# One more half-batch through VectorE and DMA, a state that decays inside PSUM, and a new order for every task of an attention-plus-mixer kernel

## The chip, the cores and the metric

The program runs on one core of a Trainium2 chip. The core has five engines with instruction streams of their own: TensorE (PE in the profile; its weight loads are listed apart as PEld), VectorE (DVE), ScalarE (ACT), GpSimd (POOL) and SyncE (SP), which here only starts DMAs. The metric is the time of one execution on the device in microseconds; lower is better. Each kernel is timed several times, and the median counts.

## The reference

The inputs are `r`, `k`, `v` of shape (4 batches, 8 heads, 768 tokens, 48), a decay `w` and a bonus `u` of shape (8, 48), and four weight matrices. All are float32, and so is the result of shape (4, 768, 384).

```python
for t in range(S):                                   # linear attention with a decaying state
    kt, vt, rt = (k[:, :, t], v[:, :, t], r[:, :, t])
    cur = np.einsum('bhd,bhe->bhde', u[None] * kt, vt)
    y[:, :, t] = np.einsum('bhd,bhde->bhe', rt, state + cur)
    state = w[None, :, :, None] * state + np.einsum('bhd,bhe->bhde', kt, vt)
...
xt = x.transpose(0, 2, 1)                            # x: the heads side by side, 384 wide
h = np.maximum(xt @ w_tok1, 0.0) @ w_tok2            # 768 -> 256 -> 768, along the tokens
u = x + h.transpose(0, 2, 1)
h2 = np.maximum(u @ w_ch1, 0.0) @ w_ch2              # 384 -> 1536 -> 384, along the channels
return u + h2
```

The `u` of the last lines is not the bonus: it is the sum of the attention's result and the token mixer's, and it is this sum that the change is about.

## The kernel before, in words

**Attention.** The 768 tokens of a batch are six units of 128 tokens. Within a unit the recurrence is turned into matrix products: `k` and `r` are multiplied by powers of `w` (tables `wnat`, `wpair`, `wp`), turned so that the channels lie on the partitions, multiplied with each other (`scores`, tile `at_ps`), masked by VectorE (`AT`), and multiplied with `v` (`outputs`, tile `y_ps`). The bonus is a separate product per head (`adg`, `yd`), and what earlier units hand on is a state of 48x48 per head, kept for two heads in one block of `kv_ps` (`state`). Batch 0 takes the units in pairs of neighbouring tokens (`pair_unit`, three windows of 256 tokens whose loads, tile `zr` or `win`, are 384 KB); batch 1 reads `r` in such windows and `k`, `v` by units; in batches 2 and 3 the scaled `k` and `r` are turned by a DMA on SP's queue (`turn_rk`).

**State.** The units of a batch are taken in groups of `GB[b]` = 2, 2, 3, 3. Inside a group the state grows in one PSUM bank (`kv_ps`), and each unit's predecessor state is copied out in bfloat16 by `keep_state`. At a group's end VectorE multiplies `kv_ps` by the decay of the whole group (`wGm`) into a tile `S0` in SBUF, and the next group begins with a product of the identity and that tile (task kinds `kv_id`, `kvw_id`), which brings the decayed state back into PSUM. There are six such ends: two each in batches 0 and 1, one each in 2 and 3.

**Mixers.** `mixer(b)` multiplies all six units of `x_b` by `wtok1` (`hidden`), takes the relu (`h1r`), and multiplies by `wtok2` (`back`). Then come two halves of three units each (`sg` 0 and 1). A half that is in `DIRECT` gets its sum `u`, channels on the partitions, wholly on PE: nine products of `x_b` with the identity turn it into `hx_ps` (`turn_x`), `back_T` adds the token mixer's part, ACT or VectorE copies the sum to `uT`, and at the very end nine more products with the identity add `uT` to the output (`down_res`). In a half that is not, `back` leaves tokens on the partitions (`hT_ps`), VectorE adds `x_b` and writes `u_sb` (`sum_u`), a DMA on SP's queue turns three units at once into `uT` (`turn_u`), and VectorE adds `u_sb` to the finished output (`sum_o`). After that both are alike: `up` makes 12 blocks `z_ps` of 1536 hidden channels (three products of 384 columns each), ACT or VectorE takes the relu into `zr`, `down` multiplies by `wch2` (tile `h_ps`, three calls of four products for each unit), and the result is stored. Batch 0 was direct in both halves, batch 1 in the first.

**Order.** Nothing is scheduled at run time. Every step is a task of class `Plan`, numbered in the order in which the code adds it; `ORDER` lists all task numbers, and `Plan.run` emits them so. Each engine therefore sees its own tasks in this order and waits for each in turn. `flex` tasks may run on one of two engines: `ENGINES` says on which. `BUFS` names the buffer that each tile takes, and a tile that takes a buffer waits until its last user is done. SP's loads stand in the same list and wait for their buffers in order; the seven pieces of the weights are DMAs of POOL, behind POOL's products.

**Zero products.** Tasks of kind `warm` multiply a tile of zeros into the unused part of PSUM bank `kv0`, as one product of 512 columns (those in `WIDE_AT`) or four of 128. Nothing waits for them. The wide ones write the whole bank and stand ahead of the first state product. Before there were 20 (10 wide).

Of the kernel before, what the change touches and what calls it, by code (L numbers as in the profile page):

```python
# [63 lines left out]
]  # L64
BUFS = {
    'AT0': [
# [1169 lines left out]
```

## Time and profile before

| | |
|---|---|
| Time, median of 3 runs | 161.94 us (161.71 to 162.23) |
| Span of the profiled execution | 160.1 us, first to last instruction |
| PE busy | 155.0 us, 97% of the span |
| VectorE busy | 116.0 us, 72% |
| ScalarE busy | 67.1 us, 42% |
| GpSimd busy | 79.0 us, 49% |
| Moved by DMA | 26.90 MB, 168 GB/s over the span |
| Granted TensorE clock | 0.997 |

The profile is of one execution, whose own span is 160.1 us; the timed median is 1.84 us above it. Busy time is the union of an engine's instructions. An engine's instructions overlap a little (products are pipelined), so a row's mean duration is longer than the step from one instruction to the next; the chain of waits gives the steps. A row of the timeline reads: start, duration, engine, line, operation, output from input, shapes, count. All operations come through one helper at line 279, so tiles, not lines, tell them apart.

### The profile page before, as it was taken

How to read it: one execution, taken by the hardware profiler on the slowest of the kernel's cores; microseconds unless marked ns; L12 is line 12 of the kernel's file. 1: busy time of each engine (PE TensorE's matmuls, PEld its weight loads, DVE VectorE, ACT ScalarE, POOL GpSimd, SP SyncE). 2: the span in 40 equal slices, each digit the busy share in tenths (PEclk: the TensorE clock that was granted, in tenths of full speed). 3: DMA queues.
4: the chain of work that ended last, by engine and by line, in shares of the span. 5: the costliest groups of instructions: out<-in, count | busy, mean ns of one | idle time of the engine just before them, and what ended most of it. 6: DMA issues, size and time to landing. Idle time of an engine off the chain costs nothing.

```text
span 160.1 us, 4053 instructions
## 1 busy us (share of the span) xinstructions
PE 155.0 (97%) x1617; PEld 105.7 (66%) x1618; DVE 116.0 (72%) x237; ACT 67.1 (42%) x149; POOL 79.0 (49%) x103
## 2 busy tenths in 40 slices
PE   6999999999999999999999999999999999999991
PEld 3577766777666777666667766676677666666670
DVE  4669995437866998879969988997797455445432
ACT  2859774976332465442316614234353200522100
POOL 7328899417145498434999917398972000000000
PEclk9999999999999999999999999999999999999998
DMA  5999999999998995899999999999961051620142
GB/s 129 262 261 244 218 233 190 198 208 195 229 212 151 188 197 112 186 153 201 207 231 152 236 131 250 220 216 151 196 168 53 0 123 26 197 84 17 49 147 98
DMA packets 86821, 26.90 MB, mean 168 GB/s; under 512 B 81554, under 2 KB 85908, under 8 KB 86804
## 3 DMA queue, kind: packets, MB, share of 16 engines
q1 hardware_dynamic: 84448, 23.40, 75.4%
q0 software_dynamic: 2160, 3.15, 11.5%
q8 instruction: 12, 0.20, 0.6%
q10 hardware_dynamic: 196, 0.11, 0.2%
q14 instruction: 5, 0.04, 0.1%
HBM read 20.46 MB, written 4.72 MB: 157 GB/s over the span
## 4 chain that ended last, share of the span: by engine, by line
PE 95%; DVE 1%; ACT 1%; issue 0%
PE h_ps L279 36%; PE z_ps L279 30%; PE kv_ps L279 8%; PE y_ps L279 6%; PE at_ps L279 4%; PE hT_ps L279 3%; PE hx_ps L279 3%; PE tr_ps L279 1%; PE w_ps L279 1%; PE trk L279 1%; ACT ka L279 1%; ACT rkb L279 1%; PE tk_ps L279 1%; PE u_ps L279 1%; PE ad_ps L279 0%; DVE pr L279 0%
## 5 line engine op out<-in xcount | busy, mean ns | idle before, releaser
L279 PE MATMUL h_ps<-wch,zr 128*128 128x384 bf16 (+1 forms) x300 | 55.0, 320 | 0.0
L279 PE MATMUL z_ps<-uT,wch 128*128 128x384 bf16 x288 | 52.0, 327 | 0.0
L279 ACT ACTIVATE zr<-z_ps 128x384 bf16<-128x384 f32 x52 | 23.6, 490 | 50.9 <-PE z_ps L279 50.8
L279 PEld LDWEIGHTS <-wch 128*128 128x128 bf16 x288 | 32.0, 114 | 13.9 <-DVE x_b L279 0.4
L279 PEld LDWEIGHTS <-zr 128*128 128x128 bf16 x300 | 27.0, 97 | 14.7
L279 DVE TENSOR_SCALAR zr<-z_ps 128x384 bf16<-128x384 f32 x44 | 23.1, 551 | 15.3 <-PE z_ps L279 15.2
L279 DVE TENSOR_TENSOR AT<-at_ps,mask 128x512 bf16<-128x512 f32 x36 | 23.2, 680 | 1.5 <-PE at_ps L279 1.5
L279 POOL TENSOR_TENSOR yd<-vb,adg 128x384 f32<-128x384 bf16 x15 | 12.6, 847 | 9.1 <-DVE vb L279 3.8
L279 POOL TENSOR_TENSOR ku<-kt,u_bc 128x384 f32<-128x384 f32 x11 | 11.0, 1001 | 11.9 <-DMA kt<-in_k_dram 9.8
L279 POOL TENSOR_TENSOR kr<-kt,wnat 128x384 bf16<-128x384 f32 x13 | 13.3, 1025 | 1.1 <-PE z_ps L279 1.0
L279 PEld LDWEIGHTS <-kr 128*128 128x128 bf16 (+1 forms) x196 | 11.7, 97 | 3.1 <-issue 0.4
L279 POOL TENSOR_TENSOR kr<-rt,wp 128x384 bf16<-128x384 f32 x10 | 10.6, 1069 | 3.1 <-DMA rt<-in_r_dram 3.1
L279 POOL TENSOR_TENSOR rku<-ku,rt 128x384 f32<-128x384 f32 x9 | 9.3, 1028 | 5.2 <-DVE adg L279 4.7
L279 DVE TENSOR_TENSOR u_sb<-x_b,hT_ps 128x384 bf16<-128x384 bf16 x15 | 7.7, 551 | 5.2 <-PE hT_ps L279 5.0
L279 PEld LDWEIGHTS <-wtok 128*128 128x128 bf16 x78 | 7.2, 98 | 4.9 <-issue 0.6
L279 DVE TENSOR_TENSOR osb<-u_sb,h_ps 128x384 f32<-128x384 bf16 (+1 forms) x16 | 8.3, 523 | 3.0 <-PE h_ps L279 2.7
L279 DVE TENSOR_TENSOR x_b<-y_ps,yd 128x384 bf16<-128x384 f32 x18 | 9.7, 552 | 0.7 <-PE y_ps L279 0.6
L279 PE MATMUL kv_ps<-warm 128*128 128x128 bf16 (+1 forms) x49 | 8.2, 328 | 1.4 <-DVE warm L279 1.4
L279 PE MATMUL h_ps<-x_b,wtok 128*128 128x384 bf16 x48 | 8.8, 327 | 0.0
L279 ACT CAST S<-kv_ps 48x192 bf16<-48x192 f32 x20 | 6.2, 312 | 4.9 <-PE kv_ps L279 3.7
L279 PE MATMUL y_ps<-vb,AT 128*128 128x48 bf16 (+1 forms) x240 | 8.2, 182 | 0.0
L279 PEld LDWEIGHTS <-warm 128*128 128x128 bf16 x50 | 4.5, 125 | 4.9 <-issue 3.3
(106 smaller groups left out, 202.9 us busy)
## 6 DMA issues: line engine op xcount, KB each, us to landing
out_dram<-osb SPq DMA_DIRECT2D x23, 192.0 KB, 2.2
vt<-in_v_dram SPq DMA_DIRECT2D x18, 192.0 KB, 4.2
kt<-in_k_dram SPq DMA_DIRECT2D x18, 192.0 KB, 4.9
rt<-in_r_dram SPq DMA_DIRECT2D x12, 192.0 KB, 3.4
wch<-in_moe_w_ch_dram POOLq DMA_DIRECT2D x4, 384.0 KB, 7.1
zr<-in_k_dram SPq DMA_DIRECT2D x3, 384.0 KB, 6.1
zr<-in_r_dram SPq DMA_DIRECT2D x3, 384.0 KB, 5.8
zr<-in_v_dram SPq DMA_DIRECT2D x3, 384.0 KB, 6.4
```

Of the source, the lines that this page charges most:

```text
L279: return lambda *args, **kw: tc.keep_in_program_order(f(*args, **kw))
```

## The change

Five things change.

1. `DIRECT` loses (1, 0): the first half of batch 1 gets its `u` from VectorE's sums and a DMA turn.
2. The state's decay at a group's end is written back into `kv_ps` by VectorE (`t_r`), and a copy to `S0` by ACT or VectorE follows as a task of its own. The six products with the identity are gone; one bank serves a whole batch. The next unit's state product waits for the copy.
3. `NWARM` is 26 instead of 20, of which 14 are wide instead of 10.
4. `ORDER`, `BUFS` and `ENGINES` are new throughout: 901 tasks instead of 891.
5. Two more columns of a table of exponents are made (`iotas`), for a table with groups of two that is not made, since no batch with DMA turns has groups of two.

```diff
-NWARM = 20
-WIDE_AT = [
-    0, 1, 2, 3, 4, 5, 6, 7, 8, 9,
-]
+NWARM = 26
+WIDE_AT = list(range(14))
...
-DIRECT = [(0, 0), (0, 1), (1, 0)]
+DIRECT = [(0, 0), (0, 1)]
...
         def add_state():
-            if g == 0:
+            if c == 0:
                 new_bank(f"kv{plan.buf('kv')}")
                 kv[0] = bank[0][:, 0:dm].rearrange("p (a q d) -> p a q d", a=HP, q=2)
-                fill(bank[0][:, 0:dm], True)
-            else:
-                fill(bank[0][:, 0:dm], False)
-            if g == 0:
-                if c > 0:
-                    pe.matmul(kv[0].rearrange("p a q d -> p (a q d)"), ident,
-                              states[b, c - 1].rearrange("p a q d -> p (a q d)"),
-                              start=True, stop=False, skip_group_check=True)
             products(kv[0])
...
                 new = sb("S0", [128, HP, 2, D], bf16)
-                dve.tensor_mul(new, kv[0], wGm[G])
+                copy(on, new, kv[0])
...
+        if c == 0:
+            owner_kv[b] = t_k = add("PE", kind, add_state, deps + [t_state.get((b - 1, C - 2))], take=("kv",), use=use)
         else:
-            t_k = add("PE", kind, add_state, deps + [t_state[b, c - 1]], use=use + [(owner_kv[b, c // G], "kv")])
...
-            t_state[b, c] = add("DVE", "x384p", lambda: keep_state("DVE"), [t_k, t_wGm[G]], take=(Sn,), use=okv)
+            t_r = add("DVE", "x384p", lambda: dve.tensor_mul(kv[0], kv[0], wGm[G]), [t_k, t_wGm[G]], use=okv)
+            t_state[b, c] = flex(EITHER, keep_state, [t_r], take=("S0",), use=okv)
...
+        iota_of(6 + 2 * NG, [[T, 2]], -T, 1)
```

Of the new lists the heads are enough to see that they are new; their entries are counted below where they are used.

```diff
 ORDER = [
-    2, 3, 26, 58, 16, 17, 57, 56, 18, 59, 0, 13, 63, 8, 884, 49, 11, 60, 14, 887, 23, 21, 1, 46, 20, 876, 4,
...
+    23, 24, 0, 57, 879, 22, 56, 3, 6, 60, 895, 893, 7, 15, 59, 18, 62, 8, 900, 27, 58, 63, 26, 13, 887, 880,
...
```

Read against the numbering of the tasks, the two lists differ in these places. The first loads were `k`, `r` of window 1, `r`, and `v` of the first window seventh; now they are `r`, `k`, two of window 1, and `v` fifth. The three `hidden` tasks of batch 0 stood between other work; now they follow each other behind the last attention of batch 0. The batch 1 units come earlier among the mixer's work of batch 0. The weight pieces 0 to 6 stood at entries 107, 159, 168, 173, 247, 260, 263 and stand at 143, 178, 183, 216, 310, 314, 347. Of the relus ACT takes 65 instead of 56 and VectorE 39 instead of 48.

More of the change, by code (lines that the diff above doesn't have):

```diff
@@ L322 @@
     krs = [const.tile([128, 2, H, P], bf16, name=f"kr{i}") for i in range(NKP)]
+    u_bc = const.tile([128, dm], f32, name="u_bc")
     ones = const.tile([1, 128], f32, name="ones")
-    u_bc = const.tile([128, dm], f32, name="u_bc")
     warm = const.tile([128, 512], bf16, name="warm")
     NW = C // 2
-    iota_i = const.tile([128, 4 + 2 + 2 * NG], i32, name="iota_i")
-    iota = const.tile([128, 4 + 2 + 2 * NG], f32, name="iota")
+    iota_i = const.tile([128, 4 + 2 + 2 * NG + 2], i32, name="iota_i")
+    iota = const.tile([128, 4 + 2 + 2 * NG + 2], f32, name="iota")
     ident_f = const.tile([128, 128], f32, name="ident_f")
@@ L497 @@
     t_ubc = once("ACT", "act384", lambda: act.copy(u_bc, U["u"]), [t_us], use=[(t_us, "m")])
-    t_wp = [decay(wp, g, 6 + NG + g, [t_io, t_wbc, t_us, t_wd, t_ud, t_uw]) for g in range(NG)]
+    TABLES = sorted({GB[n // C] for n in range(B * C) if STYLE[n][0] == "dma"})
+    wps = {3: wp}
+    t_wp = {3: [decay(wp, g, 6 + NG + g, [t_io, t_wbc, t_us, t_wd, t_ud, t_uw]) for g in range(NG)]}
+    if 2 in TABLES:
+        wps[2] = const.tile([128, 2, dm], f32, name="wnatr")
+        t_wp[2] = [decay(wps[2], g, 6 + 2 * NG + g, [t_io]) for g in range(2)]
     loaded, asked, sent = {}, {}, {}
     t_load, i_load = {}, {}
-    def wide(b):
-        return STYLE[b * C][0] in ("f32", "win")
     def two_steps(b, c, i):
-        return STYLE[b * C][0] == "win" or i == 1 and wide(b)
+        return STYLE[b * C + c][0] == "win" or i == 1 and STYLE[b * C + c][0] == "f32"
     def load(b, c, i):
@@ L635, in keep_state @@
                 new = sb("S0", [128, HP, 2, D], bf16)
-                dve.tensor_mul(new, kv[0], wGm[G])
+                copy(on, new, kv[0])
             states[b, c] = new
-        prev_S = [(t_state[b, c - 1], owner_S[b, c - 1])] if c else []
-        if g == 0:
-            t_k = add("PE", f"{kind}_id" if c else kind, add_state, deps + [t_id] + [s for s, _ in prev_S],
-                      take=("kv",), use=use + prev_S)
-            owner_kv[b, c // G] = t_k
-        else:
-            t_k = add("PE", kind, add_state, deps + [t_state[b, c - 1]], use=use + [(owner_kv[b, c // G], "kv")])
-        Sn = f"Sc{g}" if g != G - 1 else "S0"
-        okv = [(owner_kv[b, c // G], "kv")]
+        if c == 0:
+            owner_kv[b] = t_k = add("PE", kind, add_state, deps + [t_state.get((b - 1, C - 2))], take=("kv",), use=use)
+        else:
+            t_k = add("PE", kind, add_state, deps + [t_state[b, c - 1]], use=use + [(owner_kv[b], "kv")])
+        okv = [(owner_kv[b], "kv")]
         if g != G - 1:
-            t_state[b, c] = flex({"ACT": "keep", "DVE": "x384p"}, keep_state, [t_k, t_bm] + t_S0, take=(Sn,), use=okv)
-        else:
-            t_state[b, c] = add("DVE", "x384p", lambda: keep_state("DVE"), [t_k, t_wGm[G]], take=(Sn,), use=okv)
-        owner_S[b, c] = Sn
+            t_state[b, c] = flex({"ACT": "keep", "DVE": "x384p"}, keep_state, [t_k, t_bm] + t_S0, take=(f"Sc{g}",), use=okv)
+            owner_S[b, c] = f"Sc{g}"
+        else:
+            t_r = add("DVE", "x384p", lambda: dve.tensor_mul(kv[0], kv[0], wGm[G]), [t_k, t_wGm[G]], use=okv)
+            t_state[b, c] = flex(EITHER, keep_state, [t_r], take=("S0",), use=okv)
+            owner_S[b, c] = "S0"
     def unit(b, c):
@@ L727, in mul_r @@
             def mul_r(on):
-                mul(on, L["kr"][:, 1, :, 0:D], h3(loaded[b, c, 1]), h3(wp[:, g, :]))
-            t_rp = flex(PRODUCT, mul_r, [lr, t_wp[g], t_kp], use=[(lr, "rt"), (t_kp, "kp")])
+                mul(on, L["kr"][:, 1, :, 0:D], h3(loaded[b, c, 1]), h3(wps[G][:, g, :]))
+            t_rp = flex(PRODUCT, mul_r, [lr, t_wp[G][g], t_kp], use=[(lr, "rt"), (t_kp, "kp")])
             if STYLE[n][0] == "dma":
@@ L1203 @@
         if i in WIDE_AT:
-            plan.link(owner_kv[0, 0], t)
+            plan.link(owner_kv[0], t)
     plan.run()
```

102 lines of the change are left out of this document (51 added, 51 removed), and 117 rows, old and new, of tables (BUFS, ENGINES, ORDER).

## The prediction

> **What bounds the kernel now.** First the page: busy time by engine and the forty slices.
>
> ```profile
> span 160.1 us, 4053 instructions
> PE 155.0 (97%) x1617; PEld 105.7 (66%) x1618; DVE 116.0 (72%) x237; ACT 67.1 (42%) x149; POOL 79.0 (49%) x103
> PE   6999999999999999999999999999999999999991
> DVE  4669995437866998879969988997797455445432
> DMA  5999999999998995899999999999961051620142
> GB/s 129 262 261 244 218 233 190 198 208 195 229 212 151 188 197 112 186 153 201 207 231 152 236 131 250 220 216 151 196 168 53 0 123 26 197 84 17 49 147 98
> ```
>
> PE has no idle slice, so a microsecond of PE work taken out of the dense part is a microsecond of the end. But the DMA engines are nearly as full for 29 slices (to 116 us), and VectorE is full in slices 4 to 6. Where PE really waits, the busy digits don't say, since zero products count too; the chain of waits does (start, duration, what).
>
> ```profile
> 4.42 2.25 PE kv_ps L279 x11
> 7.19 2.15 PE kv_ps L279 x11
> 9.34 0.45 PE tk_ps L279 x8
> 12.52 1.01 ACT ka L279
> 14.48 0.69 DVE pr L279
> ...
> 15.82 0.42 PE at_ps L279 x15
> ...
> 28.12 0.17 PE hx_ps L279 x3
> ...
> 56.62 0.22 PE trk L279 x4
> 56.84 0.17 PE kv_ps L279 x4
> 57.01 0.82 PE h_ps L279 x7
> ...
> 61.60 0.65 PE h_ps L279 x4
> ...
> 63.78 1.95 PE h_ps L279 x12
> ...
> 67.38 0.65 PE hT_ps L279 x4
> ...
> 79.09 0.33 PE kv_ps L279 x5
> ...
> 102.58 7.34 PE z_ps L279 x45
> ...
> 156.77 0.35 DVE osb L279
> ```
>
> Until 29 us the chain changes hands between PE, ACT and VectorE; then it is PE alone until 156.77, and a sum and the last store (3.3 us) close it. So there are three parts: a **start** up to the first `back` product of batch 0, a **dense part** from there, and a tail. The timeline of the start gives its links.
>
> ```profile
> 7.43 0.49 DVE L279 TENSOR_TENSOR kr<-zr,u_sb 128x384 bf16<-128x384 f32 x1
> 16.62 0.51 PE L279 MATMUL kv_ps<-vb,kr 64*128 64x96 bf16 x8
> 18.84 0.55 DVE L279 TENSOR_TENSOR S<-kv_ps,wGm 128x384 bf16<-128x384 f32 x1
> 23.30 0.65 ACT L279 CAST S<-kv_ps 48x192 bf16<-48x192 f32 x2 [0.70 <-PE kv_ps L279]
> 24.61 0.50 PE L279 MATMUL y_ps<-S,rkb 128*128 128x96 bf16 x8
> 28.91 0.49 PE L279 MATMUL hx_ps<-wtok,h1r 128*128 128x384 bf16 x2
> ```
>
> The first product with `wtok2` starts at 28.91; from there to 156.77 are 127.9 us. The kinds of task behind it, each by its step in the chain (`up` 7.34/15 = 0.49, `down` 0.65, and so on), add up to 126.1, so such sums are good to 1.5%.
>
> **The dense part.** *The direct half.* Three `turn_x` and nine products with `uT` go. Three such products step 0.17 (28.12; and 57.01 less 61.60: 0.82 − 0.65), so −0.5 and −0.5. The six `back` products become six of `hT_ps`, 0.16 each as before: nothing. *The identity products.* A state product with one takes 0.33 (79.09), without 0.17 (56.84): −0.16, four times in this part, −0.65. *Zero products.* The list puts 24 of the 26 tasks ahead of the first `back` and two (898, 889) behind; each is four products of 128 columns, 0.22 like the four of `trk` (56.62): +0.45. Sum −1.2. One `tk`, one `sm` and a `turn_x` move ahead of the first `back` and a state product moves behind it; these cancel against the start to 0.3 and are counted there. Dense part: **−1.2**.
>
> *VectorE and ACT.* VectorE gets three sums `u_sb`, the three outputs of that half (copies before, on either engine), and one of the six new copies of the state (the lists give ACT the other five); it gives ACT nine relus. The number of decays stays six.
>
> ```profile
> L279 DVE TENSOR_TENSOR u_sb<-x_b,hT_ps 128x384 bf16<-128x384 bf16 x15 | 7.7, 551 | 5.2 <-PE hT_ps L279 5.0
> L279 DVE TENSOR_TENSOR S<-kv_ps,wGm 128x384 bf16<-128x384 f32 x6 | 3.3, 546 | 0.0
> L279 DVE TENSOR_TENSOR AT<-at_ps,mask 128x512 bf16<-128x512 f32 x36 | 23.2, 680 | 1.5 <-PE at_ps L279 1.5
> L279 ACT CAST x_b<-y_ps 128x384 bf16<-128x384 f32 x4 | 1.9, 478 | 1.5 <-PE y_ps L279 1.5
> L279 POOL IOTA iota_i<- 128x2 int32 (+1 forms) x5 | 0.6, 141 | 0.1
> uT<-u_sb SPq DMA_TRANSPOSE x5, 3.7
> ```
>
> A decay that writes float32 back into PSUM stands in no row. I bound it by the shortest row of this width (0.48, ACT's copy out of PSUM) and the row of 512 columns (0.68), and take 0.55, the row that reads the same bank and has the same shape. Six times the distance to either end is under 0.8 us, and in the dense part it lies beside PE. The copy is 0.48 on ACT, 0.55 on VectorE. The sixth `iota` is 0.14 on POOL, beside POOL's other setting up: nothing. The new wait (next state product behind decay and copy) holds up everything behind it on PE, but in batches 1 to 3 the list puts at least 2 us of `up` and `down` between: nothing, and about 0.7 each if that cover went.
>
> *The DMA turn* lands 3.7 after issue. Between the last `back` of that half and its first `up` the list has 5.9 us of `down`. Three sums (1.65), their place behind four other VectorE instructions, and 3.7 use all of it. Margin zero; if it is late, `up` waits, and behind it on SP two stores, the other half's turn, a load and a `turn_rk`. I put +0.3 for stalls here and in the next paragraph.
>
> *Batch 1 comes earlier.* The list has 26.6 us of PE work from the first `back` to batch 1's `hidden`, where the old one had 34.2 (measured 63.78 − 28.91 = 34.9).
>
> ```profile
> 28.90:63.80 34.90, 34.90 (x388) 25.04 (x385) 25.17 (x54) 19.29 (x45) 17.44 (x21) 1.00 1.05 189
> ```
>
> In that stretch VectorE was busy 25.2 us in 54 instructions; the new list has 52 in front of the same point, so about 24 us in 26.6, 91% instead of 72%. It fits, tightly.
>
> **The start.** VectorE had the first scaled `k` ready at 7.92 (7.43 + 0.49), but PE began to turn it at 9.34, behind zero products. Now 16 narrow and seven wide ones stand ahead of the first turn instead of 24 and seven, and a `tiny_mm` (0.5) moves behind it: by 7.19 (11 products, 2.15) about 1.2 us less.
>
> ```profile
> 7.43 2.92 SPq L279 DMA_DIRECT2D zr<-in_v_dram  x2
> ```
>
> Two such loads take 2.9 us, so `v` of the first window, two places earlier, lands 2.9 earlier, and the first state product (16.62) can start earlier; ahead of it stand five wide zero products and the turn of window 1. I put it at 13.5 to 15.5. From there the state of batch 0 is a chain: it took until 23.95 (23.30 + 0.65), 7.3 us, with two ends of groups in it. Each end now costs a copy (0.48) and a hand-over to ACT (about 0.15, an estimate from 18.84 + 0.55 to the next product), and saves 0.16: +0.45 each, 8.2 us in all. It ends at 21.7 to 23.7; but VectorE's 12 masks of batch 0 and ACT's casts of `v` (third window loaded one place later) stand in the same queues, so I take 23.2 to 24.4 for the third `y_ps` product, which stood at 24.61. Behind it the old order had 4.3 us to 28.91. The new one has that product (1.0), its `own4` (0.65), all three `hidden` (1.95; one stood ahead before), three `turn_x`, a `tk` and an `sm` (0.8): 4.4. So the dense part starts at 27.6 to 28.8; middle 28.2, and I take 28.5, since ACT has more in its queue there: **−0.4**. The zero products between cover waits and cost nothing; if none did, four more wide ones are 0.9.
>
> [...] The 11 products at 7.19 (three of 512 columns, eight of 128) are 2560 columns in 2.15 us, 1.2 per ns; the 45 at 102.58 are 17280 in 7.34, 2.4 per ns. PE runs at half rate in the first 9 us and at the full one from about 9.34 (1024 columns in 0.45). [...]
>
> **Sum.** 160.1 − 1.2 − 0.4 + 0.3 = 158.8 us of span; the median of the runs lies 1.84 above the span (161.94 − 160.1), so **160.6**.
>
> **The rivals.**
>
> *The start gives all it can.* If VectorE and ACT keep up, the dense part starts at 27.6 and nothing stalls: 161.94 − 1.2 − 1.3 = 159.4. For it: 2.9 us earlier `v`. Against: VectorE was full from 12 to 24 us.
>
> *The start gives it back.* The two longer ends of groups (+0.9) are not made up by the earlier loads, because the masks or the casts hold the first state product at its old place: the dense part starts at 29.8, 161.94 − 1.2 + 0.9 = 161.6, no change. For it: the third `y_ps` at 24.61 waited for the last mask and the last state alike, and the loads help one more than the other. Against: `v` is not the only thing that comes earlier; the first turn does too.
>
> *Slower: batch 1's data are late.* DMA was full throughout, and the last loads of batch 1 were slow:
>
> ```profile
> 39.70 4.02 SPq L279 DMA_DIRECT2D kt<-in_k_dram  x1
> 43.77 2.12 SPq L279 DMA_DIRECT2D vt<-in_v_dram  x2
> ...
> 36.56 1.14 POOL L279 DMA_DIRECT2D wch<-in_moe_w_ch_dram  x2
> ...
> vt<-in_v_dram SPq DMA_DIRECT2D x18, 192.0 KB, 4.2
> ```
>
> The 30th load of the old list was `v` of unit 3, issued at about 45.0 (the second of the two at 43.77) and landed 4.2 later, 49.2. It is the 30th in the new list too, behind as many bytes of loads; but its state product now stands 18.1 us of PE work behind the first `back`, at 46.6, and everything after it on PE waits. It decides from a landing later than 46.1 (a cast of 0.35 on VectorE follows); 49.2 costs 3.1. For it: the bytes are the same. Against: the last three weight pieces, 1.2 MB or 5.5 us at the 212 GB/s of slice 12, now stand later among the tasks (the old list issued the last two at 36.6, ahead of that load; the new one has them after the third window of batch 1 is scaled). If they still take a part of the queue, 2.4 us late: 160.6 + 2.4 = 163.0.
>
> *Full rate comes later.* If PE is at half rate until the zero products behind the first turns have run, about 12.5 instead of 9.3, three turns (0.45 each) and two scores (0.42 each) of batch 0 take 2.2 us more; half of that lies beside VectorE's work, so the first state product, and with it the dense part, comes 1.1 later: 161.7, no change.
>
> **How the numbers follow.** I give the forecast 0.47 (160.0 to 161.3, from a start 27.9 to 29.0 and stalls of 0 to 0.5), the full start 0.13, the start given back 0.16, late data 0.18, the late full rate 0.06. What this kernel's measurements can tell from no change is about 0.3%, 0.5 us: their own spread is 161.71 to 162.23. Faster is the first two: 0.60. Same is the start given back, the late full rate and, against them, a little of each one's edges: 0.21, rounded to 0.20. Slower is late data and what an unforeseen stall adds, 0.20. The range runs from 159.2 (full start) to 163.1 (late data at its price); the likeliest case's own is 160.0 to 161.3.
>
> **What would show it.** Each step has its row. The first product with `wtok2` starts between 27.9 and 29.0, the first state product between 13.5 and 15.5. From the first of these to the last product are 126.7 us, half a microsecond to either side. There are 62 zero products, none of `S` with the identity, 18 of `x_b` with it, 18 of `uT` with it, and six turns `uT<-u_sb`. The six decays write `kv_ps` in about 0.55. Batch 1's `hidden` (12 products `h_ps<-x_b,wtok`) starts at about 55. Late data would show as idle time of PE between 40 and 56, with POOL, ACT or VectorE waiting on `kt`, `vt` or `win`; a late turn as idle time of PE ahead of batch 1's first `z_ps`; the clock as 2560 columns still taking 2.2 us behind 9.3. The prediction is wrong if PE waits for more than 1 us in all behind 30 us, or if the first `back` comes after 29.5 with the dense part as forecast.

## The result, and the profile after

The changed kernel takes 169.21 us (median of four runs, 167.46 to 169.92) where the kernel before takes 161.94: a ratio of 1.0415, 95% interval 1.0357 to 1.0472. The forecast was 160.6, with 159.2 to 163.1 as its range. The change makes the kernel 4% slower, and none of the cases that were written down reaches that far.

The page of the changed kernel: its span, its busy times, and the forty slices of PE, VectorE, the granted clock and the DMA engines.

```profile
span 168.1 us, 4032 instructions
PE 159.0 (95%) x1606; PEld 108.3 (64%) x1606; DVE 122.0 (73%) x245; ACT 66.3 (39%) x145; POOL 79.5 (47%) x104
PE   7999789999999999988999999899999999999992
DVE  3788768593989975993998988699999574472322
PEclk9999855999999999999999999999999999999999
DMA  5999999999899940399999998998992124700223
```

PE has idle slices that it did not have before; two slices of the clock (21 to 29 us) stand at half; the DMA engines, nearly full before until 116 us, fall to 4, 0 and 3 tenths in the three slices from 58.8 to 71.4 us; and VectorE has 6 us more work (122.0 for 116.0), where the forecast listed what it gains and what it gives away without adding it up.

By the forecast's own parts: the first product with `wtok2` starts at 34.26 instead of 28.91 (+5.35); from there to PE's last product are 130.5 us instead of 127.8 (+2.7); the tail is 3.3 as before. The view by stretches, from that product to PE's end, first of the changed kernel and then of the kernel before (the columns are length, busy us and instructions of each engine, clock, DMA share, GB/s):

```profile
34.25:164.80 130.55, 127.69 (x1173) 86.56 (x1170) 98.21 (x191) 47.07 (x108) 56.14 (x59) 1.00 0.76 148
```

```profile
28.90:156.70 127.80, 127.78 (x1186) 87.29 (x1182) 94.11 (x185) 48.16 (x112) 58.32 (x63) 1.00 0.84 158
```

So the dense part has 2.86 us in which PE waits, against 0.02 before, and PE's own work in it hardly fell. Who PE waited for, in the changed kernel:

```profile
PE kv_ps L278 <- ACT S L278: 1.7, 2, 1.2
PE z_ps L278 <- DMA uT<-u_sb: 1.5, 2, 0.8
...
PE at_ps L278 <- DMA rk<-kr: 0.5, 1, 0.5
PE h_ps L278 <- DMA wch<-in_moe_w_ch_dram: 0.4, 1, 0.4
```

The first row belongs to the start, the others to the dense part. The timeline of PE in the start shows what waits there (start, duration, what, and in brackets the idle time ahead of it and what ended it):

```profile
14.67 0.51 PE L278 MATMUL kv_ps<-vb,kr 64*128 64x96 bf16 x8
...
17.96 0.38 PE L278 MATMUL kv_ps<-warm 128*128 128x128 bf16 x4 [1.24 <-ACT S L278]
...
22.91 0.59 PE L278 MATMUL kv_ps<-warm 128*128 128x128 bf16 x4 [0.43 <-ACT S L278]
...
30.20 0.50 PE L278 MATMUL y_ps<-S,rkb 128*128 128x96 bf16 x8
```

The first state product stands where the forecast put it. Then a *zero product* waits 1.24 us, until the state has been copied out. The chain of waits has the same place from the other side:

```profile
16.83 0.58 DVE kv_ps L278
...
17.43 0.49 ACT S L278
...
17.96 0.38 PE kv_ps L278 x4
```

The decay in PSUM takes 0.58, the copy 0.49, and the zero product starts 0.04 after the copy. It writes columns of the same bank that hold no state, yet it is ordered behind the copy. Nothing waits for its result, but everything behind it on PE waits with it. From about 20 us on PE then runs at half rate for 10 us: the granted clock is 0.50 in each microsecond from 20 to 30, and 44 products of `y_ps` take 2.15 us at 25.93 and 1.18 at 30.36 in that chain. That is the start. The experiments take it apart first, and the dense part afterwards.

Times below are medians; ratios are to the kernel before, run on the same chip, with 95% intervals. Some runs of both kernels were disturbed; the ratios leave those out, which is why a median and its ratio need not match.

### The profile page after: what moved, and what is told of

Same layout as the page of the kernel before. It is cut to its first block, busy times and chain, and to the rows that moved or that the text cites. A ratio compares the mean times of both kernels' runs of the same rounds, so it can differ in the third digit from the quotient of the medians.

```text
span 168.1 us, 4032 instructions
## 1 busy us (share of the span) xinstructions
PE 159.0 (95%) x1606; PEld 108.3 (64%) x1606; DVE 122.0 (73%) x245; ACT 66.3 (39%) x145; POOL 79.5 (47%) x104
## 4 chain that ended last, share of the span: by engine, by line
PE 76%; DMA 9%; DVE 8%; POOL 3%; issue 1%; ACT 1%; SPq 0%; DVEq 0%; ACTq 0%
PE h_ps L278 28%; PE z_ps L278 19%; PE kv_ps L278 8%; PE y_ps L278 6%; DMA wch<-in_moe_w_ch_dram 5%; PE at_ps L278 4%; DMA uT<-u_sb 3%; PE hT_ps L278 3%; PE tr_ps L278 2%; PE hx_ps L278 2%; DMA rk<-kr 2%; DVE u_sb L278 2%; DVE zr L278 1%; DVE kr L278 1%; DVE adg L278 1%; DVE vb L278 1%
## 5 line engine op out<-in xcount | busy, mean ns | idle before, releaser
L278 PE MATMUL h_ps<-wch,zr 128*128 128x384 bf16 (+1 forms) x300 | 51.9, 319 | 0.4 <-DMA wch<-in_moe_w_ch_dram 0.4
L278 ACT ACTIVATE zr<-z_ps 128x384 bf16<-128x384 f32 x61 | 27.8, 492 | 31.9 <-PE z_ps L278 31.7
L278 PEld LDWEIGHTS <-zr 128*128 128x128 bf16 x300 | 27.9, 98 | 16.7 <-issue 0.4
L278 DVE TENSOR_SCALAR zr<-z_ps 128x384 bf16<-128x384 f32 x35 | 18.1, 551 | 5.1 <-PE z_ps L278 5.1
L278 POOL TENSOR_TENSOR rku<-ku,rt 128x384 f32<-128x384 f32 x12 | 12.8, 1069 | 15.5 <-DVE ku L278 9.0
L278 DVE TENSOR_TENSOR osb<-u_sb,h_ps 128x384 f32<-128x384 bf16 (+1 forms) x19 | 9.9, 528 | 12.6 <-PE h_ps L278 12.5
L278 PEld LDWEIGHTS <-kr 128*128 128x128 bf16 (+1 forms) x196 | 14.0, 109 | 4.4 <-issue 1.3
L278 ACT CAST S<-kv_ps 48x192 bf16<-48x192 f32 (+1 forms) x21 | 7.4, 354 | 15.5 <-PE kv_ps L278 12.8
L278 PE MATMUL kv_ps<-warm 128*128 128x128 bf16 (+1 forms) x62 | 10.8, 332 | 2.9 <-ACT S L278 1.7
L278 POOL TENSOR_TENSOR yd<-vb,adg 128x384 f32<-128x384 bf16 x11 | 9.1, 841 | 9.0 <-ACT vb L278 4.5
L278 DVE TENSOR_TENSOR AT<-at_ps,u_sb 128x512 bf16<-128x512 f32 x12 | 8.0, 684 | 2.1 <-PE at_ps L278 1.6
L278 POOL TENSOR_TENSOR kr<-rt,wp 128x384 bf16<-128x384 f32 x7 | 7.1, 1011 | 4.5 <-DMA rt<-in_r_dram 4.5
```

What stands on the lines that cost most here:

```text
L278: return lambda *args, **kw: tc.keep_in_program_order(f(*args, **kw))
```

## Experiment 1: three zero products moved

Three zero product tasks go a few tasks later in the list, behind tasks that need no state.

```diff
+MOVED = [(896, 171), (890, 201), (891, 320)]
+for _n, _behind in MOVED:
+    ORDER.remove(_n)
+    ORDER.insert(ORDER.index(_behind) + 1, _n)
```

> The changed kernel with three of the zero product tasks of the start moved a few tasks later in the list, each behind a task that needs no state (scores of window 1, scores of window 2, the turn of unit 0 of batch 1); nothing else. Theory A, the zero products hold PE up: they write into the bank that holds the state, so each waits until the state has been copied out (1.24 us at 17.96, 0.43 at 22.91), everything behind them on PE waits too, and the gap takes the clock away. Then PE should not stand idle for more than 0.5 us in all between 16 and 24 us, the granted clock should stay at 1.0 from 9 us on, the first product with wtok2 should start at 29.5 to 31.5 instead of 34.26, and the time should be 164 to 166.5 us. Theory B, decaying in place and copying is a longer chain and the zero products only stand where its gaps are: the same idle time appears before other products, the first product with wtok2 stays at 33 to 34.5, and the time is within 1 us of 169.2.

Measured: 165.53 us, ratio 1.0166 (1.0099 to 1.0233), granted clock 0.997 or more in every run. PE's timeline of this run:

```profile
18.15 0.33 PE L284 MATMUL y_ps<-S,rkb 128*128 128x96 bf16 x4
...
24.89 0.50 PE L284 MATMUL y_ps<-S,rkb 128*128 128x96 bf16 x8
29.13 0.81 PE L284 MATMUL hx_ps<-wtok,h1r 128*128 128x384 bf16 x4
```

The first product with `wtok2` comes at 29.13, 0.22 us behind the kernel before (theory A had allowed 29.5 at the earliest), and 5.1 earlier than in the changed kernel, by nothing but the place of twelve products that add zero. Theory A holds, and theory B falls: PE stood idle for 0.28 us between 16 and 24, the state's chain was the same, and the third `y_ps` product started at 24.89 instead of 30.20. But of the 5.1 us only some 4 reach the end:

```profile
PE z_ps L284 <- DMA uT<-u_sb: 1.6, 2, 0.9
...
PE at_ps L284 <- DMA rk<-kr: 1.2, 1, 1.2
PE z_ps L284 <- DMA wch<-in_moe_w_ch_dram: 1.2, 1, 1.2
PE h_ps L284 <- DMA wch<-in_moe_w_ch_dram: 0.4, 1, 0.4
```

A dense part that starts earlier waits longer for the weight pieces and the turns of `rk`: these rows add up to 4.4 us, those of the changed kernel's dense part to 2.4.

## Experiments 2 and 3: the state's part of the change undone, and done alone

Undone: the changed kernel's list with the state code of before (the decay goes straight to the bf16 state and enters the next bank by an identity product). The identity product comes back and the task numbers shift with it; the diff shows the decay only.

```diff
-            t_r = add("DVE", "x384p", lambda: dve.tensor_mul(kv[0], kv[0], wGm[G]), [t_k, t_wGm[G]], use=okv)
-            t_state[b, c] = flex(EITHER, keep_state, [t_r], take=("S0",), use=okv)
+            t_state[b, c] = add("DVE", "x384p", lambda: keep_state("DVE"), [t_k, t_wGm[G]], take=(Sn,), use=okv)
```

> The changed kernel with the state handled as before: the decay is written straight to the bf16 state and enters the next window's bank by an identity product; no copy behind the decay. Order, zero products and the DMA-turned half as in the changed kernel. Theory A (zero products that wait for the bank): the bank is free 0.5 us earlier, so the 1.24 us gap shrinks to 0.5 to 0.8 and the clock may or may not stay; first product with wtok2 at 31 to 34, time 166 to 169. Theory B (the longer chain): three waits of about 0.6 go and with them the clock loss, first product with wtok2 at 29 to 31, time 164 to 166. By both, the stalls behind 48 us stay (about 2.8 us) and four identity products add 0.65 behind the first product with wtok2.

Measured: 166.40 us, ratio 1.0253 (1.0129 to 1.0376), clock 0.999 or more. The first product with `wtok2` is at 30.72, and the zero products still wait, only for less long:

```profile
17.20 0.38 PE L210 MATMUL kv_ps<-warm 128*128 128x128 bf16 x4 [0.72 <-DVE S L210]
...
21.57 0.38 PE L210 MATMUL kv_ps<-warm 128*128 128x128 bf16 x4 [0.45 <-ACT S L210]
```

The time is what theory A gave (166 to 169), with the gap at 0.72; the first product with `wtok2` came earlier than it gave, inside theory B's window, because the clock stayed. This run alone would not have decided between them.

Done alone: the kernel before with the new state code, each copy listed directly behind its decay, everything else as before.

```diff
 DIRECT = [(0, 0), (0, 1), (1, 0)]
-            t_state[b, c] = add("DVE", "x384p", lambda: keep_state("DVE"), [t_k, t_wGm[G]], take=(Sn,), use=okv)
+            t_r = add("DVE", "x384p", lambda: dve.tensor_mul(kv[0], kv[0], wGm[G]), [t_k, t_wGm[G]], use=okv)
+            t_state[b, c] = flex(EITHER, keep_state, [t_r], take=("S0",), use=okv)
```

> The kernel before with one part of the change alone: the state is decayed in place in PSUM and copied out, the six identity products go, each copy stands directly behind its decay in the list; order, engines, zero products and batch 1's half as before. In this order no zero product stands between a state product and its copy. Theory A (the in-place decay is harmless where no zero product waits on its bank): four identity products less in the dense part, -0.65, two less and two copies more in the start, +0.3 to +0.9; time 161.4 to 162.4 where the kernel before takes 161.9. Theory B (decay and copy are a chain that the start cannot hide): the first product with wtok2 at 30.5 or later instead of 28.91, time 163 to 165.

Measured: median 164.19 us, ratio 0.9988 (0.9942 to 1.0034), no difference. PE's work in the dense part fell from 127.78 to 127.36 us. The profiled execution was one of the longer ones (164.47): its first product with `wtok2` is at 31.65, inside theory B's window, so this profile does not settle the start, and the verdict rests on the ratio. By it, in an order without zero products between state and copy the in-place decay neither helps nor hurts; the edit that looked like the risk is not what costs.

## Experiments 4 and 5: the waits put into the other order

To put the wait into the kernel before, the decays and copies of batch 0 must stand directly behind their state products, as the changed kernel lists them. That alone is the control.

```diff
+MOVED = [(150, 149), (151, 150), (178, 177), (208, 207)]
```

> The control for the next run: the kernel before with the in-place decay, and each decay, copy and cast of batch 0's state listed directly behind its state product (as the changed kernel lists them); no zero product is moved. The state's chain can only come earlier by this, other work of VectorE and ScalarE a little later: first product with wtok2 at 28.5 to 30 in a run whose loads are on time, time 161 to 163, granted clock 1.0.

Measured: 166.16 us, ratio 1.0273 (1.0224 to 1.0322). The control was expected to change nothing, and it lost 4 us. Its timeline, PE and then ScalarE:

```profile
18.66 0.51 PE L216 MATMUL kv_ps<-vb,kr 64*128 64x96 bf16 x8
20.48 0.33 PE L216 MATMUL y_ps<-S,rkb 128*128 128x96 bf16 x4 [1.31 <-ACT adg L216]
```

```profile
19.87 0.48 ACT L216 CAST S<-kv_ps 128x384 bf16<-128x384 f32 x1 [2.91 <-DVE kv_ps L216]
20.25 0.18 ACT L216 COPY adg<-ad_ps 128x16 f32<-128x16 f32 x1
```

ScalarE now meets the state's copy first and stands 2.91 us before it, waiting for the decay; the small copy `adg`, which the list before had ahead of it, comes behind, and PE waits 1.31 us for that. Again one gap of about 1.3 us near 19 us, and again the clock falls (0.967 to 0.979 in the four runs; in the profile from 23.4 us on, 3 us behind the gap): the first product with `wtok2` comes at 33.66. So the gap need not come from a zero product: here a small copy held up in ScalarE's queue made it.

Then the three zero product tasks are moved behind the copies:

```diff
+MOVED = [(150, 149), (151, 150), (178, 177), (208, 207)]
+MOVED += [(894, 151), (895, 178), (896, 208)]
```

> The control with three of its early zero product tasks moved behind the copy of the second state and the casts of the third and fifth, as the changed kernel has them. Theory A (zero products that write the state's bank wait for the copy and hold PE up): PE waits 0.8 to 1.3 us on the second state's copy and 0.2 to 0.5 on the others, the first product with wtok2 comes 1.2 to 2 us later than in the control, more if the clock is taken away, and the time is 1.2 to 4 us above the control's. Theory B (the order or the chain was to blame, not these products): within 0.5 us of the control.

Measured: 170.94 us, ratio 1.0553 (1.0466 to 1.0639), 4.8 us above its control, more than theory A gave. The first product with `wtok2` comes at 38.05, 4.4 behind the control's, and the clock is lower too (0.96 to 0.98). The waits are those of the changed kernel, in a list that is otherwise the old one:

```profile
20.06 0.59 PE L217 MATMUL kv_ps<-warm 128*128 128x128 bf16 x4 [1.24 <-ACT S L217]
...
23.52 0.58 PE L217 MATMUL kv_ps<-warm 128*128 128x128 bf16 x4 [0.74 <-ACT S L217]
...
29.55 0.58 PE L217 MATMUL kv_ps<-warm 128*128 128x128 bf16 x4 [0.79 <-ACT S L217]
```

## Experiment 6: the zero products of the start left out

Five zero product tasks, all between the first state product and the first product with `wtok2`, are not issued. They add nothing to any sum, so the output does not change.

```diff
+for _n in (896, 892, 890, 899, 891):
+    ORDER.remove(_n)
```

> The changed kernel without the five zero product tasks between the first state product and the first product with wtok2 (20 products of 128 columns). If the clock went because of the gap that they made: first product with wtok2 at 28.3 to 29.5, granted clock 0.99 or more, 164.5 to 166.5 as with the three moved. If PE needs their work to keep its clock there: the waits of PE are gone but the clock falls all the same, 0.96 to 0.98, first product with wtok2 at 31 to 34, 167 to 169.

Measured: median 167.15 us (164.60 to 168.63). The ratio, 1.0137 (1.0041 to 1.0233), rests on the two of five executions whose clock stayed at 0.999 or more; the other three, at 0.98 to 0.99, took 167.15 to 168.63. In the profiled one, the longest, the first product with `wtok2` is at 28.78, the earliest of all profiles, and the clock dips twice:

```profile
PEclk9999969996999999999999999999999999999999
```

Neither theory holds alone. The gap is gone and the start is early, as the first has it; but the clock falls all the same in three executions. The first dip (22 to 25 us) comes 2 us behind a microsecond in which PE was busy 0.42, with no wait above 0.50 us; the second (39 to 42) follows a wait of 2.4 us for a weight piece. So leaving the zero products out is not shown to be better than moving them.

## Experiments 7 to 10: the dense part, and who makes the turn late

The half turned by PE again, each task put where the changed kernel's list has the one that it replaces:

```diff
-DIRECT = [(0, 0), (0, 1)]
+DIRECT = [(0, 0), (0, 1), (1, 0)]
```

> The changed kernel with the first half of batch 1's u formed and turned by PE again (turn by identity, back products, copy), each put where the changed list has the product or sum it replaces; the rest of the list is unchanged. Theory C, the DMA turn is late (1.5 us of waits of the products with uT at 73.8 and 78.2): the first wait goes, the second stays or shrinks, PE gets 1.0 us more work, so 168 to 169.2. Theory D, the sums and the turn are late only because VectorE's and SP's queues are (casts of v of 1 us each, SP blocked from 59 to 66 us): the second half's turn is late as before, both waits together stay above 1 us, and the time is 169.2 to 170.5.

Measured: 168.14 us, ratio 1.0357 (1.0262 to 1.0453), not to be told from the changed kernel's 1.0415. PE's work in the dense part is 128.59, 0.9 more than in the changed kernel; of the two waits for `uT` one of 1.3 us stays, as theory D has it. The time lies below theory D's window and inside theory C's, but it does not decide: in the profiled run the clock was at half for 3.4 us instead of 10. The second half's turn is late whoever forms the first.

The chain of waits of the changed kernel names what stands ahead of that turn; the second view is its SP queue.

```profile
66.58 0.56 DVE u_sb L278
...
67.59 0.46 DVE u_sb L278
68.06 1.97 DVE vb L278 x2
70.03 1.85 DVE u_sb L278 x4
...
73.00 5.14 DMA uT<-u_sb
```

```profile
56.27 2.84 SPq L278 DMA_DIRECT2D kt<-in_k_dram  x1
66.36 1.33 SPq L278 DMA_TRANSPOSE rk<-kr  x1
70.52 1.28 SPq L278 DMA_TRANSPOSE uT<-u_sb  x1
71.89 1.02 SPq L278 DMA_DIRECT2D out_dram<-osb  x2
73.00 1.30 SPq L278 DMA_TRANSPOSE uT<-u_sb  x1
```

Two casts of `v` for batch 2 stand between the sums of `u` on VectorE and take 2 us; five of this kernel's six other such casts take 0.34 or 0.35 each. SP issues nothing from 59.1 to 66.36: the first turn of `rk` stands next in its queue and waits 7.2 us for VectorE's scaled tile `kr`. That is why the DMA engines are empty there. Two runs ease these queues, one around the late zero products and one with them moved:

```diff
+MOVED = [(38, 406), (39, 38), (53, 39), (516, 540), (298, 429), (308, 298)]
+for _i, _e in [(166, 0), (172, 0), (171, 0), (181, 0)]:
+    ENGINES[_i] = _e
```

> The changed kernel with its zero products where they are, and only the queues around batch 1's turns eased (two casts of v to ScalarE, two products to GpSimd, three decay tables earlier, two stores behind the second turn). Theory D (VectorE's and SP's queues make the turns late): the two waits of the products with uT, 1.5 us, go; 167.2 to 168.5 where the changed kernel took 169.2. Rival: with the late start the data of batch 2 are early enough anyway and the waits come from the 3.7 us of the turn itself: 168.8 to 169.6, waits as before.

> The run with the three zero product tasks moved, and the queues around batch 1's turns eased: two casts of v of batch 2 go from VectorE to ScalarE, two products of batch 2 from VectorE to GpSimd, three decay tables are computed by ScalarE before batch 1's relu, and two stores stand behind the second turn of batch 1's u in SP's queue. Theory D (VectorE's and SP's queues make the turns late, not the turn itself): the waits of the products with uT (1.6 us together at 69 and 73 us) shrink below 0.5, the DMA engines are not idle for 12 us between 56 and 72, and the time is 162.8 to 164.6 where the run with moved zero products alone took 165.5. Theory C (3 to 5 us of DMA turn have no cover in this order): the waits stay at 1.2 us or more, time 165 to 166.

Measured: alone 167.66 us, ratio 1.0335 (1.0251 to 1.0418); with the zero products moved 164.31, ratio 1.0140 (1.0080 to 1.0200). In both the waits for `uT` are gone, and in both a new one stands, 1.4 us for a scaled `k` of batch 1 on VectorE. The run with the zero products left where they were shows one thing more. Its profiled execution kept the full clock (1.00) with the same gap:

```profile
18.36 0.38 PE L286 MATMUL kv_ps<-warm 128*128 128x128 bf16 x4 [1.24 <-ACT S L286]
...
32.41 0.81 PE L286 MATMUL hx_ps<-wtok,h1r 128*128 128x384 bf16 x4
```

The first product with `wtok2` stands at 32.41, between the 29.13 of experiment 1 and the 34.26 of the changed kernel. By that, some 3 of the 5.1 us are the waits of the zero products and some 2 the clock, an estimate from these three profiles. Part of what this run gains on the changed kernel is the clock as well, which stayed at 1.00 in two of its four executions and in one of the changed kernel's.

Then the two casts alone go to ScalarE, which in the changed kernel was idle there (4.46 us, from 67.06 to 71.52), with the zero products moved:

```diff
 MOVED = [(896, 171), (890, 201), (891, 320)]
+for _i, _e in [(166, 0), (172, 0)]:
+    ENGINES[_i] = _e
```

> The run with the three zero product tasks moved, and of the eased queues only the two casts of v of batch 2 given to ScalarE. VectorE spends 2.0 us on them beside GpSimd's products (0.35 each elsewhere), between the second and third sum of the first half. If VectorE alone sets the turns: both turns are issued 1.5 to 2 us earlier, the waits on uT fall from 1.6 to below 0.5, 164.0 to 165.0. If SP's order (the turn of rk that waits for a product, the two stores between the turns) sets them: the first wait shrinks, the second stays at 0.5 to 0.9, 165.0 to 165.8.

Measured: 163.32 us, ratio 1.0100 (1.0066 to 1.0134), below what was expected of it. Its waits:

```profile
PE z_ps L286 <- DMA wch<-in_moe_w_ch_dram: 1.2, 1, 1.2
PE hx_ps L286 <- DMA wtok<-in_moe_w_tok_dram: 0.2, 1, 0.2
```

No wait for `uT` is left, with SP's order untouched (the two stores still stand between the turns). Both turns are issued 2.4 us earlier than in experiment 1 (64.3 and 66.8 us, there 66.7 and 69.2). So VectorE's two casts, not SP's order, made the turns late. The slower of the two turns also landed 3.4 us after its issue, where experiment 1's took 5.2; no run shows why.

## Experiments 11 to 15: the weight pieces, and what is left

The last three pieces issued directly behind the fourth, in the changed kernel:

```diff
+for _n, _behind in ((123, 122), (124, 123), (125, 124)):
+    ORDER.remove(_n)
+    ORDER.insert(ORDER.index(_behind) + 1, _n)
```

> The changed kernel with the last three weight pieces issued directly behind the fourth instead of behind POOL's products for batch 1 (from 48.3 us on). Theory E, the late pieces bind: the wait of 0.41 us for a piece at 56.7 goes, batch 0's down products run earlier, and the time falls by 0.4 to 1.5 us. Theory F, the pieces take the queues from batch 1's loads if they go early (as the order of the kernel before suggests, where loads of 5 to 10 us stood beside them): PE then waits for kt, vt or win between 40 and 56 us and the time rises by 0.5 to 2.5 us.

Measured: 169.48 us, against 169.21. The wait of 0.41 us is gone, as theory E says, and in the three executions that lost the clock (0.967 to 0.970), like most of the changed kernel's, the time is not lower (169.34 to 170.19): PE still waits 1.6 us for `uT` behind it. The one that kept it took 165.76, where the changed kernel's one took 167.46; one execution of each does not settle a gain.

All pieces earlier, with the zero products moved, and then with the queues eased as well:

```diff
+MOVED += [(120, 170), (121, 120), (122, 121), (123, 326), (124, 349), (125, 124)]
```

> The run with the three zero product tasks moved, and the weight pieces issued at about the points of GpSimd's work where the kernel before has them: the second, third and fourth behind its last product of own terms for window 1, the fifth to seventh behind its products for batch 1's first two windows. Theory E (late pieces bind once the start is repaired): the wait of 1.18 us of the first up for a piece at 37.9 and the 0.4 of the first down go, time 163.6 to 164.8. Theory F (early pieces starve the loads of batch 1): waits for kt, vt or win of 0.5 to 3 us appear between 36 and 56, time 165 to 168.

> Both repairs on top of the moved zero products. If the two sets of waits are independent their gains add: 161.0 to 163.5, with less than 1.5 us of waits of PE behind 30 us. If the removal of one only uncovers the next (VectorE's masks, the rk turns, the loads), the gain is that of the better one or less: 163.5 to 165.5, and the waits name other tiles than wch and uT.

Measured: 170.01 us, ratio 1.0476 (1.0434 to 1.0519), and 166.55 us, ratio 1.0237 (1.0171 to 1.0303), where the runs without the early pieces had 1.0166 and 1.0140. The first is clearly worse; the second's interval overlaps a little. Theory F holds: in the first of them one load of batch 1's window takes SP 8.78 us to issue, from 32.41 on, after GpSimd issued pieces at 28.13 and 30.66 (in experiment 1 such a load takes 1.39 to 2.88), and PE waits 2.7 us for the `k` that is behind it.

```profile
27.70 4.67 SPq L285 DMA_DIRECT2D vt<-in_v_dram  x1
32.41 8.78 SPq L285 DMA_DIRECT2D win<-in_r_dram  x1
```

Last, from the run with zero products moved and casts on ScalarE: the two zero product tasks of the dense part left out; and with that, only the fourth piece issued earlier, directly behind the third.

```diff
+for _n in (889, 898):
+    ORDER.remove(_n)
```

> The same without moving the weight piece: the control for it, and against the run with moved zero products and casts on ScalarE (163.3) the price of two zero product tasks in the dense part. If they cost PE's time as counted, 0.45 less: 162.7 to 163.0. One of them (0.22) stands directly behind the eighth to tenth up, where PE waits for the weight piece anyway; if it and the other lie in such a wait's shadow, nothing: 163.1 to 163.5.

```diff
+MOVED += [(122, 121)]
```

> The changed kernel with the three zero product tasks moved, the two casts of v on ScalarE, the two zero product tasks behind the first product with wtok2 left out, and the fourth weight piece issued directly behind the third, 3.6 us earlier. Theory E (the piece binds): the wait of 1.2 us ahead of the eighth up shrinks to 0 to 0.4, no new wait above 0.5 us appears, 161.2 to 162.3. Theory F (two pieces together starve batch 1's loads): waits for kt, vt or win of 0.5 to 2 us between 36 and 48, 162.6 to 165.

Measured: 163.50 us, ratio 1.0049 (1.0010 to 1.0089), and 163.01 us, ratio 1.0010 (0.9962 to 1.0058). PE's work in the dense part went from 127.35 to 126.91 us with the two tasks out, which is 0.44 where 0.45 was counted; in the time it is not settled, since the interval overlaps that of the run before it. The last repair brings the changed kernel level with the kernel before; its interval and its neighbour's overlap, so the piece's own share is not settled either. Nor do the profiles settle it: the wait of 1.2 us for the piece was down to 0.2 in the neighbour's profile, with the piece where it was, and the repaired run's profile, of a long execution (164.73), waits 1.7 us for a piece of `wtok`. No version beat the kernel before.

## Why the prediction was wrong, point by point

**The start, "the zero products between cover waits and cost nothing".** This is the step that failed, and it is most of the loss. The forecast asked what the new chain of decay and copy costs the next *state product*, 0.45 at each end of a group, and found cover for it. It did not ask what else on PE depends on the bank. Zero products do: three of them were listed behind copies, two of them waited 1.24 and 0.43 us for them in the profile, and held PE's queue. So a term put at nothing was worth 5.1 us at the first product with `wtok2`. The rest of the start's sum was nearly sound: the first state product at 14.67 (forecast 13.5 to 15.5), and with the zero products moved the third `y_ps` at 24.89 (forecast 23.2 to 24.4) and the first product with `wtok2` at 29.13 (27.9 to 29.0), 28.78 without those products. In the chain of the changed kernel both zero products start 0.04 us after a copy of other columns of their bank (17.96 after 17.92, 22.91 after 22.87); state and zeros are also one tile of the program here, and no run shows whether bank or tile orders them.

**"Full rate comes later", given 0.06.** The rival was about the first full rate. No run shows its 12.5; in the changed kernel the full rate came in time (1024 columns take 0.85 us at 8.67 and 0.55 at 10.36). The clock was lost later: behind a gap of 1.24 us in the changed kernel PE ran at half rate for 10.2 us, behind one of 1.31 in the control of experiment 4 for 6.8. Without a gap above 0.72 it stayed in the profiled runs of experiments 1 and 2. The gap does not decide alone: with the same 1.24 us the clock stayed in one of the four timed runs of the changed kernel and in the profiled run that eased the queues with the zero products in place, and in experiment 6 it went at 22 us without one. The changed kernel's run that kept it was its fastest (167.46 against 168.98 to 169.92), so the clock is worth some 2 us there, an estimate from these four times, and the waits the rest. The gap of 1.24 stands in a stretch where PE was busy 2.76 us of 4, as the view by stretches of the changed kernel has it (columns as above).

```profile
16.00:20.00 4.00, 2.76 (x84) 2.33 (x82) 2.68 (x7) 2.31 (x4) 3.16 (x4) 0.98 1.18 237
```

**"An identity product −0.16 each, −0.65 in all".** Measured by doing it alone: −0.42 of PE's work in the dense part, and no time that can be told. The decay in place takes 0.561 (0.55 taken), the copy 0.484 (0.48).

**"The direct half −0.5 and −0.5".** Putting it back on PE adds 0.9 to PE's work. The sign and size were right. **"Zero products +0.45"**: 0.44.

**The dense part, −1.2.** PE's work in it fell by 0.1 in the changed kernel and by 0.43 where most of the waits were gone (127.35). By the three terms as measured it should be 0.9; where the other 0.45 went is open.

**"The DMA turn, margin zero: +0.3".** 1.5 us of waits for the turns instead, and 2.86 for all of PE's waits in the dense part, which the same +0.3 was to cover. This is the second term that was mis-sized. The margin was reckoned with the four VectorE instructions in front at their usual durations. Two of them are casts, and they took 0.98 and 1.15 instead of 0.35, beside GpSimd's products. The view of that tile in the changed kernel (least, median and most ns of the two casts, first and last start), and GpSimd's timeline there:

```profile
L278 DVE CAST vb<-vt x2: 977/1065/1153, 68.0 to 68.9; 128x384 bf16<-128x384 f32 x2
```

```profile
67.74 1.00 POOL L278 TENSOR_TENSOR rku<-ku,rt 128x384 f32<-128x384 f32 x1 [0.58 <-DVE adg L278]
68.69 1.11 POOL L278 TENSOR_TENSOR ku<-kt,u_bc 128x384 f32<-128x384 f32 x1
```

The forecast counted three sums gained and nine relus given away; it missed that the lists also put eight casts of `v` on VectorE where there were three, 3.5 us of the 6 us by which its work grew:

```profile
L278 DVE CAST vb<-vt 128x384 bf16<-128x384 f32 x8 | 4.5, 568 | 0.0
```

```profile
L279 DVE CAST vb<-vt 128x384 bf16<-128x384 f32 x3 | 1.0, 350 | 0.0
```

Of the eight casts five took 0.34 or 0.35 us, four of them with no GpSimd product beside them and one beside the last 0.1 us of one; the three others (0.68, 0.98 and 1.15) each ended 0.21 or 0.22 us behind the end of a GpSimd product. No run takes GpSimd's products away, so the cause is not shown.

**Batch 1's `hidden` at 55.** It came at 62.31, 28.0 us behind the first product with `wtok2` instead of 26.6.

**"Late data", given 0.18, with the later weight pieces as an argument against it.** Half right; it is not what made the loss. Early pieces do hold up batch 1's loads (with all pieces earlier one load took 8.78 us to issue, PE waited 2.7 us for the `k` behind it, and the ratio was 1.0476, where it was 1.0166 without: +5 us). But late ones bind PE too, which the forecast did not weigh: 0.41 us in the changed kernel and 1.2 where the start was repaired. With batch 1 brought forward by 7.6 us of PE work, loads and weights want the same DMA time (in the changed kernel the DMA engines stand at 8 or 9 tenths from 4.2 to 58.8 us), and both orders lose.

**What would show it wrong** was stated: more than 1 us of PE's waits behind 30 us, or a first `back` after 29.5. Both limits were passed, with 2.9 us and 34.26. The ends of the range, 159.2 and 163.1, lie 0.2 and 0.1 outside what their own cases add up to (159.4 and 163.0); that changes nothing here.

## What to carry to other kernels

A filler is an instruction like any other: list what it writes, who else uses that bank or tile, and where it stands in its queue, before it is costed at nothing; here one such product waited 1.24 us for a copy. In a stretch where PE has little to do, ask of every wait not only how long it is but how little work it leaves PE around it: here PE was busy 2.76 us of 4 around that wait, and in that profile ran at half rate for 10.2 us behind it. When lists are made anew, count what each engine gained per kind of instruction, not only the kinds that the change speaks of, and where two engines work side by side take the duration measured there: 0.98 and 1.15 us for a cast that otherwise took 0.35.

## What the runs showed of the hardware that was not expected

A gap of about 1.3 us near 18 to 20 us mostly went with a loss of PE's full clock, but not always. Six of the kernels profiled had it (the changed kernel, the control of experiment 4 and its partner, and the three runs that leave the changed kernel's start as it is); in 20 of their 24 timed runs the granted clock was 0.96 to 0.99, in four 1.00. With gaps of 0.72, 0.45 and 0.24 us in a row it stayed at 0.999 or more in all four runs of experiment 2; in experiment 6, with no gap above 0.50 in the start, it fell in three of five, in the profiled one at 22 us and once more behind a wait of 2.4. Each stretch at half rate lasted close to a multiple of 3.4 us: 3.4 in the run with the half on PE and twice in experiment 6, 6.8 in the control, 10.2 in the changed kernel, 13.6 in the control's partner (from the granted clock of each microsecond). No run shows what sets these lengths, or why a gap costs the clock in one execution and not in another.

The same cast of 128x384 from float32 to bf16 took VectorE 0.35 us with no GpSimd product beside it, and 0.68, 0.98 and 1.15 beside one. And in the run with all pieces earlier a load on SP's queue took 8.78 us to issue, from 32.41 on, after GpSimd had issued weight pieces at 28.13 and 30.66.
